# A planned kernel of attention and two MLPs: another DMA model in the planner, other places in the order for weight conversion

## The chip, the cores and the metric

One core of one Trainium2 chip. The time is the device time of one execution in microseconds (us); the median of several executions is compared. The engines are named as the profile names them: PE (TensorE, matmuls), DVE (VectorE), ACT (ScalarE), POOL (GpSimd), SP (SyncE, which here only issues DMAs).

## The reference

Windowed attention over 4 batches, 8 heads, 576 positions, head size 64: heads 0 to 3 see the last 32 positions, heads 4 to 7 every fourth of the last 128. Its output, 2304 tokens by 512, goes through two MLPs:

```python
scores = np.where(masks, scale * np.matmul(q, k.transpose(0, 1, 3, 2)), -1e9)
x = np.matmul(softmax(scores), v)            # (2304, 512) after the heads are joined
h = x @ w_in                                 # first MLP, d_ff 2048
x = (h * np.cos(h)) @ w_out
gate = 1.0 / (1.0 + np.exp(-(x @ w_gate)))   # second MLP, d_ff 1536
out = (gate * (x @ w_val)) @ w_out2
```

The result is float32.

## The kernel before

**Arithmetic.** The matmuls of the MLPs use fp32r operands. A number is split into a high part and a rest, and a product is three matmuls (lines 747 to 749 for the first MLP, 1054 to 1056 and 1202 to 1204 for the second). Weights come as raw bits of wider numbers and are converted on the chip: per weight block of 128x512 a load (403 or 406), ACT's `low` (410) and `mag` (419, or 417 on DVE), then DVE's `shift` (422), `top` (425) and `rnd` (433). For the second MLP there follow, per pair of blocks, four differences on DVE (480, for a scheme that saves one of eight block products), ACT's high part (488), POOL's rest (492) and four DMAs that save the result to DRAM (497). It is read back when its section comes (1029 for gate and value weights, 1188 for the output weights).

**Stages.** The first stage is attention, which feeds the first MLP chunk by chunk (six chunks of 384 tokens). The first MLP has 96 steps: 48 over the first half of d_ff and 48 over the second half, eight steps to a chunk. A step n is the group `h` (12 matmuls into a bank `ps_h`), a chain that alternates between ACT and DVE (`turn` 797 on ACT, `part` 801 on DVE, `cos` 804 on ACT, `g` 807 on DVE, `g_hi` 814 on ACT or 812 on DVE, `g_lo` 817 on DVE), and the group `x2` (12 matmuls into four accumulator banks). After a chunk's last step DVE or ACT takes the four banks out (`x2_take`, 877 on DVE in the second half, 881 and 883 in the first), and only then can the next chunk's first `x2` begin. Weight conversion for the second MLP lies beside these steps. The second MLP has 36 sections, twelve for each pair of chunks; a section has seven products (`p`, into two banks called ps_x, ps_y, ps_z in turn). DVE adds them up in the order u2, u3, vb (1072), gate_b (1083), va (1072) and two `mul` (1090). PE's fourth product waits for u2, its sixth for u3, its seventh for vb, and the next section's first for the bank that gate_b frees. Sums and splits for the output product are DVE's 1161 and 1181.

**What sets the order.** The class `Plan` (lines 55 to 230) is a list scheduler in Python that runs when the kernel is built. Every task has an engine, a duration in ns, dependencies, buffers that it takes and gives, and a priority `prio` in units of steps. The planner plays the tasks through in its own time, an engine that is free takes the ready task of lowest `prio`, and emits each instruction in that order. On the chip each engine, SP too, then works through its queue strictly in that order, and a late instruction holds back all behind it. `port=True` marks tasks that the planner doesn't let run on DVE and POOL at once. `NUDGE` shifts priorities of kinds of tasks while these are under 16 (attention and the first steps). `W_GATE` holds back conversion: gate and value block j may load from step 38 + 1.5 j on, output blocks from step 72 + 1.6 j on (j counted from the first of them). While the first chunk is not yet through, the planner fills idle time of PE with small matmuls, `warm` (1317), of 128x128 bf16; their number is fixed when the kernel is built.

**DMAs in the planner.** Before, some transfers (attention's inputs, raw weights, `x_save`) go through a modelled server `line`, one transfer after another; all others are an SP duration plus a fixed latency, as 3 n ns and 3500 ns for a save of converted weights, or 1460 and 4500 for the read of output weights.

Of the kernel before, what the change touches and what calls it, by code (L numbers as in the profile page):

```python
# [37 lines left out]
SEC = 2.75  # L38
W_PRIO, W_START = 4.5, -4
W_GATE = (12.0, 1.8, 38.0, 1.5, 72.0, 1.6)  # L40
# [6 lines left out]
NUDGE = {"head": 7, "k_out": 1, "load_qk": -0.75, "load_v": -0.75, "p_out": 0.75, "p_transp": -0.5, "pv": -3.5, "s_eps":  # L47
         1, "s_exp": 0.75, "s_max": -0.25, "s_norm": -3.75, "s_rec": 0.5, "scores": 0.5, "w": -0.75, "w_hi": -0.25, "w_load":
         -0.25, "w_mag": 0.5, "w_top": -3.5, "x": 0.75, "x_hi": -1.75}
# [3 lines left out]
class Plan:  # L53
# [18 lines left out]
    DMA_START = 3100  # L72
# [27 lines left out]
    def run(self, start):  # L100
# [35 lines left out]
        while left:  # L136
# [8 lines left out]
            for e in ready:  # L145
# [11 lines left out]
                for k in order:  # L157
# [67 lines left out]
def windowed_attention_mlp_kernel(ctx, tc, q, k, v, w_in, w_out, w_gate, w_val, w_out2, out):  # L225
# [528 lines left out]
    def x_tasks(c):  # L754
# [20 lines left out]
        if c < NC - 2:  # L775
# [4 lines left out]
            add(("x_again", c), "sp", 4400, again, [("x_save", c), prev], begin[s - 1] + 4.0, take=["x"], lat=2200)  # L780
# [84 lines left out]
    def x2_out(s, c, half, n, i):  # L865
# [21 lines left out]
        if half:  # L887
# [5 lines left out]
            add(("x2_load", s, i), "sp", 550, load, [("x2_save", order.index(c), i), "late"] + old, p - 4, take=["o"] if tag == "o" else [], lat=3200,  # L893
# [4 lines left out]
        add(("x2_save", s, i), "sp", 550, lambda: SP.dma_start(out=(x2d if half else x2h)[c][:, i, :], in_=st["o"]),  # L898
            [("x2_take", s, i)], p, give=["o"] if tag == "o" else [], lat=3200 if half else 2200)
# [13 lines left out]
    def xs_tasks(s):  # L913
# [7 lines left out]
        for kk in range(2):  # L921
# [24 lines left out]
            for i, nm in enumerate(("b0", "b1", "a0", "a1")):  # L946
                c, k = (2 * s if nm[0] == "a" else 2 * s + 1), 2 * int(nm[1]) + kk
                deps = [("x2_save", NC + c, k), "late"]
                add(key("xs_load", nm), "sp", 550, lambda nm=nm, f=load: f(nm), deps, base - 1 + i * 0.01, take=["xt"], lat=4200, gate=gate,
# [24 lines left out]
    def xs_wide(s, ca, cb):  # L974
# [22 lines left out]
        for i in range(2):  # L997
            deps = [("x2_save", NC + 2 * s + i, k) for k in range(KD)] + ["late"] + free
            add(("xw_load", s, i), "sp", 1500, lambda i=i: load(i), deps + ([("xw_load", s, 0)] if i else []), base - 1, lat=6000, gate=base - 2)
# [21 lines left out]
    def mlp2_tasks(n):  # L1021
# [9 lines left out]
        for c in (0, 2, 1, 3):  # L1031
# [8 lines left out]
            add(("w2", n, c), "sp", m * 1.5, lambda a=(c, o, m): w_load(*a), deps, p - 2 * SEC + c * 1e-3, lat=2600)  # L1040
# [107 lines left out]
    def out2_tasks(s):  # L1148
# [58 lines left out]
        for j, (nm, _, _) in enumerate(PRODS):  # L1207
            for m in range(NM):
                q = j * NM + m
                whole = end and j == len(PRODS) - 1  # L1210
                if q % 2 == 0:
# [4 lines left out]
                    else:  # L1216
                        deps = [o_key(s, q - 6 + 1)] if g >= 3 else [o_key(s - 1, 42 - 6 + q + 1)] if s else w_saved
                    add(("ow", s, g), "sp", 1460, lambda q=q: w_load(q), deps + [("w2_save", F2 + z, i) for z in range(NM) for i in range(4)],
                        o_pr(q) - (3 if end else 2) * O_LEAD, lat=4500, after=[("ow", s, g - 1)] if g else [])
# [21 lines left out]
                add(("o", s, q), "pe", 9 * 116, lambda a=(j, m): [mm(*a, i) for i in range(TT)], deps, o_pr(q), take=take)  # L1241
            if whole:
                for i in range(TT):
                    deps = [("o_lo", s, nm, m) for m in range(NM)] + [("ow", s, g) for g in range(18, 21)] + [o_key(s, 35 + i)] + (o_read(s, j) if i == 0 else [])
                    add(("o", s, 36 + i), "pe", 18 * 116, lambda i=i: [mm(6, m, i) for m in range(NM)], deps, o_pr(36 + i))
# [14 lines left out]
    def out_tasks(s, j, i, deps, pr):  # L1260
# [30 lines left out]
        if saved:  # L1291
            add(("o_save", s, saved, i), "sp", 550, lambda: save(saved, k), [(what, s, i)], pr, lat=2200)
# [76 lines left out]
```

## Time and profile before

| | |
|---|---|
| median of 3 runs | 946.66 us (943.94 to 952.67) |
| profiled execution | 944.66 us |
| span in the profile | 942.9 us |
| busy PE, DVE, ACT, POOL | 925.6, 718.1, 494.1, 186.7 us |
| PE matmuls | 6952 |
| busy share of the 16 DMA engines, main queue | 72.4% |

A busy time is the sum of an engine's instructions with overlaps counted once. Idle time on PE has a releaser, the instruction for which it waited. A mean duration of a matmul (336 ns for 128x384) is longer than the distance between two starts, since matmuls overlap.

### The profile page before, as it was taken

To read this page: it belongs to the slowest core of one execution; us is meant where nothing else is said; L and a number is where in the kernel's file an instruction comes from. 1 tells how busy PE (TensorE), PEld (TensorE's weight loads), DVE (VectorE), ACT (ScalarE), POOL (GpSimd) and SP (SyncE) were. 2 spreads that over 40 slices of the span, in tenths; PEclk is the share of its full clock that TensorE was granted. 3 is DMA by queue.
4 is the path that set the end of the run, shared out by engine and by line. 5 is a ranking of instruction groups with operands and counts; after the bars stand their busy time and mean duration, and the time that the engine had idled before them with its cause. 6 is when DMAs were issued, how large, how long until landed. Compare 5 with 4: busy or idle time off the path is not lost. (4 is left out here: it accounts for less than half of the span.)

```text
span 942.9 us, 19301 instructions
## 1 busy us (share of the span) xinstructions
PE 925.6 (98%) x6952; PEld 899.9 (95%) x6952; DVE 718.1 (76%) x1720; ACT 494.1 (52%) x1188; POOL 186.7 (20%) x208
## 2 busy tenths in 40 slices
PE   8999999999999999999998999999999999999998
PEld 7889999998999999999998999999999999999998
DVE  6888678787768969998999875776666796566683
ACT  5887678766776466555655522243333253332261
POOL 4434132232223333423422420000000000000000
PEclk9999999999999999999999999999999999999999
DMA  8966545555235699788887698977888987887593
GB/s 194 228 194 183 151 127 152 161 131 145 58 104 178 210 344 335 280 317 297 307 296 236 232 377 294 334 242 238 263 271 274 319 310 244 266 267 215 188 324 109
DMA packets 160911, 221.47 MB, mean 235 GB/s; under 512 B 60592, under 2 KB 126896, under 8 KB 159792
## 3 DMA queue, kind: packets, MB, share of 16 engines
q1 hardware_dynamic: 160016, 220.05, 72.4%
q8 instruction: 55, 0.90, 0.4%
q14 instruction: 40, 0.33, 0.1%
q10 hardware_dynamic: 800, 0.20, 0.1%
HBM read 166.72 MB, written 53.48 MB: 234 GB/s over the span
## 5 line engine op out<-in xcount | busy, mean ns | idle before, releaser
L492 POOL TENSOR_TENSOR lr<-lf,lr 128x512 fp32r<-128x512 f32 (+1 forms) x72 | 92.7, 1306 | 172.0 <-ACT lr L488 159.8
L747 PE MATMUL acc<-gs,arena 128*128 128x384 f32 x240 | 84.8, 353 | 0.9 <-ACT o L883 0.9
L749 PE MATMUL acc<-gs,arena 128*128 128x384 f32 x240 | 80.8, 336 | 0.0
L748 PE MATMUL acc<-gs,arena 128*128 128x384 f32 x240 | 80.6, 336 | 0.0
L1054 PE MATMUL ps_y<-arena 128*128 128x384 f32 x216 | 73.6, 341 | 2.4 <-DVE u L1072 1.8
L1056 PE MATMUL ps_y<-arena 128*128 128x384 f32 x216 | 72.8, 337 | 0.0
L1055 PE MATMUL ps_y<-arena 128*128 128x384 f32 x216 | 72.7, 337 | 0.0
L817 DVE TENSOR_TENSOR gs<-u,gs 128x384 fp32r<-128x384 f32 x96 | 63.7, 666 | 10.3 <-ACT gs L814 9.9
L804 ACT ACTIVATE u<-u 128x384 f32<-128x384 f32 x96 | 49.8, 523 | 40.1 <-DVE u L801 38.8
L797 ACT ACTIVATE r<-ps_h 128x384 int32<-128x384 f32 x96 | 46.4, 483 | 44.4 <-PE ps_h L749 44.0
L747 PE MATMUL ps_h<-arena 128*128 128x384 f32 x192 | 68.4, 356 | 0.6 <-DVE u L807 0.6
L801 DVE SCALAR_TENSOR_TENSOR u<-ps_h,r 128x384 f32<-128x384 f32 x96 | 52.9, 551 | 20.3 <-ACT r L797 19.7
L807 DVE TENSOR_TENSOR u<-ps_h,u 128x384 f32<-128x384 f32 x96 | 52.5, 550 | 17.7 <-ACT u L804 17.4
L749 PE MATMUL ps_h<-arena,wb 128*128 128x384 f32 x192 | 64.7, 337 | 0.0
L748 PE MATMUL ps_h<-arena,wb 128*128 128x384 f32 x192 | 64.7, 337 | 0.0
L747 PE MATMUL ps_h<-arena,wb 128*128 128x384 f32 x192 | 64.7, 337 | 0.0
L749 PE MATMUL ps_h<-arena 128*128 128x384 f32 x192 | 64.5, 336 | 0.0
L748 PE MATMUL ps_h<-arena 128*128 128x384 f32 x192 | 64.4, 335 | 0.0
L1087 ACT ACTIVATE sg<-sg 128x384 f32<-128x384 f32 x36 | 18.9, 525 | 84.3 <-DVE sg L1083 84.3
L410 ACT ACTIVATE wst<-wst 128x512 int32<-128x512 uint32 x68 | 46.1, 677 | 31.0 <-DMA wst<-in_moe_w_val_dram 11.3
L646 ACT ACTIVATE s<-s,mx 128x80 f32<-128x80 f32 (+1 forms) x168 | 59.3, 357 | 0.7 <-DVE mx L639 0.6
L747 PE MATMUL acc<-gs,wb 128*128 128x384 f32 x144 | 49.8, 346 | 4.9 <-DVE lf L877 3.6
(201 smaller groups left out, 2951.3 us busy)
## 6 DMA issues: line engine op xcount, KB each, us to landing
arena<-wd SPq DMA_DIRECT2D x108, 512.0 KB, 4.6
lr<-od SPq DMA_DIRECT2D x42, 512.0 KB, 4.6
wd<-lr SPq DMA_DIRECT2D x36, 512.0 KB, 4.7
wst<-in_moe_w_out_dram SPq DMA_DIRECT2D x28, 512.0 KB, 4.5
arena<-od SPq DMA_DIRECT2D x21, 512.0 KB, 5.6
arena<-wd SPq DMA_DIRECT2D x36, 256.0 KB, 3.9
od<-lr SPq DMA_DIRECT2D x18, 512.0 KB, 4.9
wst<-in_moe_w_in_dram SPq DMA_DIRECT2D x16, 512.0 KB, 4.5
```

The lines of the kernel that those rows point to most:

```text
L492: POOL.tensor_tensor(out=l, in0=x, in1=h.bitcast(F32), op=ALU.subtract)
L646: ACT.activation(out=s, in_=s, func=AF.Exp, scale=-1.0, bias=row("mx", u)[:, i:i + 1], accum_out=row("rs", u)[:, i:i + 1])
L747: PE.matmul(ps, wh, xl, start=first, stop=False)
L748: PE.matmul(ps, wl, xh, start=False, stop=False)
L749: PE.matmul(ps, wh, xh, start=False, stop=last)
L801: DVE.scalar_tensor_tensor(st["u"], st["h"], INV_2PI, st["r"], op0=ALU.mult, op1=ALU.subtract)
L804: ACT.activation(out=st["u"], in_=st["u"], func=AF.Sin, scale=TWO_PI, bias=HALF_PI)
L807: DVE.tensor_tensor(out=st["u"], in0=st["h"], in1=st["u"], op=ALU.mult)
L817: DVE.tensor_tensor(out=st["gs"][:, 1, :], in0=st["u"], in1=st["gs"][:, 0, :].bitcast(F32), op=ALU.subtract)
L1054: PE.matmul(st[to], wh, xl, start=first, stop=False, **more)
L1055: PE.matmul(st[to], wl, xh, start=False, stop=False, **more)
L1056: PE.matmul(st[to], wh, xh, start=False, stop=kk == 1, **more)
```

## The change

All transfers now go through the planner's one server, each with a time by its size, and landing at the earliest `DMA_LEAD` = 2200 ns after its issue plus that time; SP's own cost of an issue is 450 ns everywhere. The first loads keep their formula. Planned durations of the output products rise from 116 to 118.5 ns a matmul. Conversion for the second MLP may start two steps earlier and somewhat closer together. The table of nudges is another. No instruction is added or removed but `warm` matmuls, 267 instead of 298, and a handful of conversion steps that change between ACT and DVE.

```diff
-W_GATE = (12.0, 1.8, 38.0, 1.5, 72.0, 1.6)
+W_GATE = (12.0, 1.8, 36.0, 1.4, 70.0, 1.6)
...
-NUDGE = {"head": 7, "k_out": 1, "load_qk": -0.75, "load_v": -0.75, "p_out": 0.75, "p_transp": -0.5, "pv": -3.5, "s_eps":
...
+NUDGE = {"head": 4.5, "k_out": 0.75, "load_qk": -0.75, "load_v": 3.75, "p_out": -2, "p_transp": -2.5, "pv": -3.75,
...
-    DMA_START = 3100
+    DMA_START, DMA_LEAD = 3100, 2200
+    FIRST_LOADS = ("load_qk", "load_v", "w_load", "x_save")
...
-                        line = max(line, end - t["dma"] + self.DMA_START) + t["dma"]
+                        line = max(line, end + (self.DMA_START - t["dma"] if k[0] in self.FIRST_LOADS else self.DMA_LEAD)) + t["dma"]
...
-            add(("w2_save", nw, z), "sp", 3 * n, lambda a=(k0, k1): save(*a), [("w_blo", nw, z)], pr, lat=3500)
+            add(("w2_save", nw, z), "sp", 450, lambda a=(k0, k1): save(*a), [("w_blo", nw, z)], pr, dma=3 * n)
...
-                        o_pr(q) - (3 if end else 2) * O_LEAD, lat=4500, after=[("ow", s, g - 1)] if g else [])
+                        o_pr(q) - (3 if end else 2) * O_LEAD, dma=1600, after=[("ow", s, g - 1)] if g else [])
...
-                add(("o", s, q), "pe", 9 * 116, lambda a=(j, m): [mm(*a, i) for i in range(TT)], deps, o_pr(q), take=take)
+                add(("o", s, q), "pe", 9 * 118.5, lambda a=(j, m): [mm(*a, i) for i in range(TT)], deps, o_pr(q), take=take)
```

The other changed calls (`x_again`, `x2_load`, `x2_save`, `xs_load`, `xw_load`, `w2`, `o_save`) exchange a duration and `lat` for 450 and `dma` in the same way. In the changed kernel each line after `FIRST_LOADS` stands one further down.

**Place 1: DVE where the last chunk but one ends (steps 88 to 91 of the first MLP).** Line 877 (878 after) takes out the accumulator banks, L801 is `part` of step 90, and after the change L802 is that of step 91. Before:

```order
L801 SCALAR_TENSOR_TENSOR u<-ps_h,r 128x384
L480 TENSOR_TENSOR lf<-lf 128x256
L425 SCALAR_TENSOR_TENSOR wc<-wst,wc 128x512
L480 TENSOR_TENSOR lf<-lf 128x256
L807 TENSOR_TENSOR u<-ps_h,u 128x384
L877 TENSOR_TENSOR lf<-acc_6487,lf 128x384
L877 TENSOR_TENSOR lf<-acc_6494,lf 128x384
L877 TENSOR_TENSOR o<-acc_6498,o 128x384
L877 TENSOR_TENSOR o<-acc_6505,o 128x384
```

After:

```order
L878 TENSOR_TENSOR lf<-acc_6469,lf 128x384
L878 TENSOR_TENSOR lf<-acc_6478,lf 128x384
L481 TENSOR_TENSOR lf<-lf 128x256
L808 TENSOR_TENSOR u<-ps_h,u 128x384
L818 TENSOR_TENSOR gs<-u,gs 128x384
L481 TENSOR_TENSOR lf<-lf 128x256
L939 TENSOR_TENSOR arena<-xt,arena 128x384
L423 TENSOR_SCALAR wc<-wc 128x512
L939 TENSOR_TENSOR arena<-xt,arena 128x384
L802 SCALAR_TENSOR_TENSOR u<-ps_h,r 128x384
L878 TENSOR_TENSOR o<-acc_6484,o 128x384
L878 TENSOR_TENSOR o<-acc_6498,o 128x384
```

The first two takes moved from behind three conversion instructions and `g` of step 90 to right behind `part` of step 90 (the row ahead of those shown); the other two now stand behind `part` of step 91.

**Place 2: DVE between sections 3 and 4 of the second MLP.** The first row is the end of section 3 (`mul`), the L1072 (L1073) is u2 of section 4, for which PE waits. Before:

```order
L1090 TENSOR_TENSOR ub<-u_7405,sg 128x384
L1161 TENSOR_TENSOR ub<-ub 128x384
L1181 TENSOR_TENSOR ur<-ub,ur 128x384
L1161 TENSOR_TENSOR ub<-ub 128x384 x2
L1181 TENSOR_TENSOR arena<-ub,arena 128x384
L1161 TENSOR_TENSOR ub<-ub 128x384
L1072 TENSOR_TENSOR u_7480<-ps_y,s_7458 128x384
```

After:

```order
L1091 TENSOR_TENSOR ub<-u_7380,sg 128x384
L1162 TENSOR_TENSOR ub<-ub 128x384 x2
L1073 TENSOR_TENSOR u_7448<-ps_y,s_7435 128x384
L1073 TENSOR_TENSOR sg<-ps_y,s_7435 128x384
L1182 TENSOR_TENSOR ur<-ub,ur 128x384
L1073 TENSOR_TENSOR vb<-ps_z,sg 128x384
L1162 TENSOR_TENSOR ub<-ub 128x384
L1084 TENSOR_TENSOR sg<-ps_y,s_7435 128x384
```

Of the six sums and splits (1161, 1181) ahead of u2, two are left; the others stand further down, between the additions of section 4.

**Place 3: DVE in section 0, between u2 (the row right ahead of these) and u3 (the L1073 at the end), after the change.** Before, the same stretch held seven conversion instructions and two takes.

```order
L939 TENSOR_TENSOR arena<-xt,arena 128x384
L423 TENSOR_SCALAR wc<-wc 128x512
L939 TENSOR_TENSOR arena<-xt,arena 128x384
L426 SCALAR_TENSOR_TENSOR wc<-wst,wc 128x512
L418 TENSOR_SCALAR wc<-wst 128x512
L434 ISA lf<-wst,wc 128x1024
L423 TENSOR_SCALAR wc<-wc 128x512
L481 TENSOR_TENSOR lf<-lf 128x256
L426 SCALAR_TENSOR_TENSOR wc<-wst,wc 128x512
L481 TENSOR_TENSOR lf<-lf 128x256
L434 ISA lf<-wst,wc 128x1024
L1073 TENSOR_TENSOR sg<-ps_y,s_7063 128x384
```

Nine conversion instructions and two splits now stand ahead of u3, and the takes behind it.

## Rows read from the trace of the kernel before

**Rows 1.** The page, part 1: busy time, share of the span, instructions of each engine

```profile
PE 925.6 (98%) x6952; PEld 899.9 (95%) x6952; DVE 718.1 (76%) x1720; ACT 494.1 (52%) x1188; POOL 186.7 (20%) x208
```

**Rows 2.** Waits of PE over the span: total us, times, longest us

```profile
PE acc L747 <- DVE lf L877: 3.6, 2, 3.3
...
PE ps_y L1054 <- DVE u L1072: 1.8, 1, 1.8
...
PE acc L747 <- ACT o L883: 1.5, 2, 0.9
PE acc L747 <- DVE o L881: 0.7, 1, 0.7
```

**Rows 3.** Windows: busy us of each engine by stretch, granted clock, DMA share

```profile
core 0: us, PE busy (x) PEld busy (x) DVE busy (x) ACT busy (x) POOL busy (x), PEclk, DMA share, GB/s
...
60.00:80.00 20.00, 20.00 (x209) 18.95 (x207) 18.73 (x48) 18.30 (x50) 8.77 (x9) 1.00 0.50 138
...
505.00:510.00 5.00, 4.00 (x15) 4.00 (x16) 3.87 (x9) 3.46 (x8) 1.84 (x2) 0.66 0.67 246
```

**Rows 4.** Timeline of PE, 45 to 48 us: start, duration, line, operation, count

```profile
45.96 1.45 PE L1317 MATMUL acc<-identb 128*128 128x128 bf16 x23
47.25 0.50 PE L597 MATMUL ps_t<-ident,k 96*128 96x96 f32 x4
```

**Rows 5.** Timeline of PE, 500 to 509 us

```profile
500.49 0.34 PE L747 MATMUL ps_h<-arena,wb 128*128 128x384 f32 x1
...
502.40 0.34 PE L749 MATMUL ps_h<-arena,wb 128*128 128x384 f32 x1
506.00 0.69 PE L747 MATMUL acc<-gs,wb 128*128 128x384 f32 x1 [3.26 <-DVE lf L877]
...
509.00 0.34 PE L747 MATMUL acc<-gs,wb 128*128 128x384 f32 x1
```

**Rows 6.** Timeline of DVE, 501 to 515 us

```profile
501.50 0.41 DVE L480 TENSOR_TENSOR lf<-lf 128x256 f32<-128x256 f32 x1
501.84 1.78 DVE L425 SCALAR_TENSOR_TENSOR wc<-wst,wc 128x512 int32<-128x512 int32 x1
503.54 1.48 DVE L480 TENSOR_TENSOR lf<-lf 128x256 f32<-128x256 f32 x1
...
505.40 1.01 DVE L877 TENSOR_TENSOR lf<-acc,lf 128x384 f32<-128x384 f32 x2
...
514.91 0.68 DVE L425 SCALAR_TENSOR_TENSOR wc<-wst,wc 128x512 int32<-128x512 int32 x1
```

**Rows 7.** Timeline of POOL, 500 to 507 us

```profile
501.59 5.25 POOL L492 TENSOR_TENSOR lr<-lf,lr 128x512 fp32r<-128x512 f32 x4 [11.51 <-ACT lr L488]
```

**Rows 8.** Timeline of PE, 567 to 574 us

```profile
567.91 0.34 PE L1056 MATMUL ps_x<-arena 128*128 128x384 f32 x1
570.04 0.44 PE L1054 MATMUL ps_y<-arena 128*128 128x384 f32 x1 [1.79 <-DVE u L1072]
...
573.80 0.34 PE L1054 MATMUL ps_y<-arena 128*128 128x384 f32 x1
```

**Rows 9.** Timeline of DVE, 566 to 570 us

```profile
566.33 0.55 DVE L1161 TENSOR_TENSOR ub<-ub 128x384 f32<-128x384 f32 x1
...
569.44 0.55 DVE L1072 TENSOR_TENSOR u<-ps_y,s 128x384 f32<-128x384 f32 x1
```

**Rows 10.** Timeline of PE and, under it, of DVE before 558 us

```profile
555.13 0.34 PE L1056 MATMUL ps_z<-arena 128*128 128x384 f32 x1
557.28 0.44 PE L1054 MATMUL ps_x<-arena 128*128 128x384 f32 x1 [1.81 <-DVE sg L1083]
...
555.14 1.62 DVE L1161 TENSOR_TENSOR ub<-ub 128x384 f32<-128x384 f32 x1
556.69 0.54 DVE L1083 TENSOR_TENSOR sg<-ps_y,s 128x384 f32<-128x384 f32 x1
```

**Rows 11.** The page, part 6: DMA issues, median us from issue to landing

```profile
lr<-od SPq DMA_DIRECT2D x42, 512.0 KB, 4.6
```

More of the change, by code (lines that the diff above doesn't have):

```diff
@@ L46 @@
 NUDGE_UNTIL = 16
-NUDGE = {"head": 7, "k_out": 1, "load_qk": -0.75, "load_v": -0.75, "p_out": 0.75, "p_transp": -0.5, "pv": -3.5, "s_eps":
-         1, "s_exp": 0.75, "s_max": -0.25, "s_norm": -3.75, "s_rec": 0.5, "scores": 0.5, "w": -0.75, "w_hi": -0.25, "w_load":
-         -0.25, "w_mag": 0.5, "w_top": -3.5, "x": 0.75, "x_hi": -1.75}
+NUDGE = {"head": 4.5, "k_out": 0.75, "load_qk": -0.75, "load_v": 3.75, "p_out": -2, "p_transp": -2.5, "pv": -3.75,
+         "q_out": -0.5, "s_eps": 2.75, "s_exp": 1, "s_max": -1, "s_norm": -1.25, "s_rec": 3.5, "scores": -4.5, "transp": -0.25,
+         "w_hi": -0.25, "w_load": 0.5, "w_mag": 2, "w_rnd": -0.5, "x": -10.25, "x_hi": -3.75, "x_save": -8.5}
 WARM, WARM_NS = 1200, 57
@@ L779, in x_tasks @@
             prev = ("x_again", order[s - 1]) if s > NC + 2 else ("x_new", NC - 1)
-            add(("x_again", c), "sp", 4400, again, [("x_save", c), prev], begin[s - 1] + 4.0, take=["x"], lat=2200)
+            add(("x_again", c), "sp", 450, again, [("x_save", c), prev], begin[s - 1] + 4.0, take=["x"], dma=4600)
         add(("x_free2", c), None, 0, nothing, [("h", last, KD - 1)], give=["x"])
@@ L892, in x2_out @@
                 xr_slots.append(("x2_save", s, i))
-            add(("x2_load", s, i), "sp", 550, load, [("x2_save", order.index(c), i), "late"] + old, p - 4, take=["o"] if tag == "o" else [], lat=3200,
+            add(("x2_load", s, i), "sp", 450, load, [("x2_save", order.index(c), i), "late"] + old, p - 4, take=["o"] if tag == "o" else [], dma=600,
                 after=xr_prev("x2_load", s, i))
@@ L897, in x2_out @@
             give=["acc" if i < 3 else "accw"])
-        add(("x2_save", s, i), "sp", 550, lambda: SP.dma_start(out=(x2d if half else x2h)[c][:, i, :], in_=st["o"]),
-            [("x2_take", s, i)], p, give=["o"] if tag == "o" else [], lat=3200 if half else 2200)
+        add(("x2_save", s, i), "sp", 450, lambda: SP.dma_start(out=(x2d if half else x2h)[c][:, i, :], in_=st["o"]),
+            [("x2_take", s, i)], p, give=["o"] if tag == "o" else [], dma=600)
     order2 = order[NC:]
@@ L948, in xs_tasks @@
                 deps = [("x2_save", NC + c, k), "late"]
-                add(key("xs_load", nm), "sp", 550, lambda nm=nm, f=load: f(nm), deps, base - 1 + i * 0.01, take=["xt"], lat=4200, gate=gate,
+                add(key("xs_load", nm), "sp", 450, lambda nm=nm, f=load: f(nm), deps, base - 1 + i * 0.01, take=["xt"], dma=600, gate=gate,
                     after=prev + ([key("xs_load", ("b0", "b1", "a0")[i - 1])] if i else []))
@@ L998, in xs_wide @@
             deps = [("x2_save", NC + 2 * s + i, k) for k in range(KD)] + ["late"] + free
-            add(("xw_load", s, i), "sp", 1500, lambda i=i: load(i), deps + ([("xw_load", s, 0)] if i else []), base - 1, lat=6000, gate=base - 2)
+            add(("xw_load", s, i), "sp", 450, lambda i=i: load(i), deps + ([("xw_load", s, 0)] if i else []), base - 1, dma=2400, gate=base - 2)
         loads = [("xw_load", s, 0), ("xw_load", s, 1)]
@@ L1039, in mlp2_tasks @@
                 deps.append(("h", (begin[2 * NC - 1] if c else NSTEP) - 1, KD - 1))
-            add(("w2", n, c), "sp", m * 1.5, lambda a=(c, o, m): w_load(*a), deps, p - 2 * SEC + c * 1e-3, lat=2600)
+            add(("w2", n, c), "sp", 450, lambda a=(c, o, m): w_load(*a), deps, p - 2 * SEC + c * 1e-3, dma=m * 1.5)
         def mm(j, kk):
@@ L1217, in out2_tasks @@
                         deps = [o_key(s, q - 6 + 1)] if g >= 3 else [o_key(s - 1, 42 - 6 + q + 1)] if s else w_saved
-                    add(("ow", s, g), "sp", 1460, lambda q=q: w_load(q), deps + [("w2_save", F2 + z, i) for z in range(NM) for i in range(4)],
-                        o_pr(q) - (3 if end else 2) * O_LEAD, lat=4500, after=[("ow", s, g - 1)] if g else [])
+                    add(("ow", s, g), "sp", 450, lambda q=q: w_load(q), deps + [("w2_save", F2 + z, i) for z in range(NM) for i in range(4)],
+                        o_pr(q) - (3 if end else 2) * O_LEAD, dma=1600, after=[("ow", s, g - 1)] if g else [])
                 k = slots[q % len(slots)]
@@ L1244, in out2_tasks @@
                     deps = [("o_lo", s, nm, m) for m in range(NM)] + [("ow", s, g) for g in range(18, 21)] + [o_key(s, 35 + i)] + (o_read(s, j) if i == 0 else [])
-                    add(("o", s, 36 + i), "pe", 18 * 116, lambda i=i: [mm(6, m, i) for m in range(NM)], deps, o_pr(36 + i))
+                    add(("o", s, 36 + i), "pe", 18 * 118.5, lambda i=i: [mm(6, m, i) for m in range(NM)], deps, o_pr(36 + i))
             for i in range(TT):
@@ L1291, in out_tasks @@
         if saved:
-            add(("o_save", s, saved, i), "sp", 550, lambda: save(saved, k), [(what, s, i)], pr, lat=2200)
+            add(("o_save", s, saved, i), "sp", 450, lambda: save(saved, k), [(what, s, i)], pr, dma=400)
     xy, zz = {}, {}
```

## The prediction

> **What bounds the kernel now.** I read the busy times first: PE works in 98% of the span, DVE in 76%, ACT in 52% [rows 1]. The change takes away no work of DVE or ACT, and of PE only filler, so it can gain just what PE loses: 17.3 us of idle time in the span (942.9 less 925.6), some filler, and time at a lower clock. The waits of PE then show for whom it idles [rows 2]: for accumulator banks that DVE takes out (3.6 us) or ACT and DVE in the first half (1.5 and 0.7), and for u2 in the second MLP (1.8). No DMA is among the large ones. Nearly all of it lies in few places, and I read those in the timelines.
>
> Place 1, at 506 us. PE's last matmul of step 91's `h` starts at 502.40, its next at 506.00 [rows 5]. The usual distance is 1.91 / 11 = 0.174 us (from 500.49 to 502.40), so 506.00 - 502.57 = 3.43 are lost. The following nine matmuls take 3.00 us to the next start at 509.00 instead of 9 x 0.174 = 1.57: the granted clock in that stretch is 0.66 on average, so part of it ran at 1.2 GHz instead of 2.4, right after the idle time [rows 3]. Together 4.9 us. The take came at 505.40 because two conversion instructions ahead of it lasted 1.78 and 1.48 us [rows 6], where the same forms take 0.68 and 0.41 elsewhere in these rows. POOL ran four of its 128x512 subtractions from 501.59 for 5.25 us [rows 7]. So some 2.2 of the 3.4 us is DVE held up beside POOL, and the rest is DVE's order.
>
> Place 2, at 570 us. PE stands from 568.08 to 570.04 (1.96), and its next twelve matmuls take 3.76 us to 573.80 instead of 2.09 [rows 8]: together 3.6 us. DVE does six sums and splits from 566.33 before it reaches u2 at 569.44 [rows 9]. POOL has finished by then; this is order alone.
>
> At 557 us PE loses 557.28 - 555.30 = 2.0 us behind gate_b, which stood behind a sum of 1.62 us against 0.55 for the same form in [rows 9], again beside POOL [rows 10]. The two waits for ACT and DVE in the first half's takes [rows 2] sum to 2.2, of which I count 1.3 at the change from the first to the second half of d_ff and 0.9 earlier. That makes 12.7 us in named places. The rest of the idle time is the first wait of the program, the tail, and pieces under 0.7.
>
> **What the change does, term by term.** I start from the profiled execution, 944.66 us (span 942.9 and 1.8 around it).
>
> Filler: 31 `warm` matmuls fewer. They stand in PE's own queue and are executed whatever happens, at 1.29 / 23 = 0.056 us each [rows 4]: -1.7 us, if nothing else makes PE wait there. That holds the planner's word that attention runs more tightly; the bounds are 0, if DVE is late by as much, and -1.7.
>
> Place 1: the first two takes now stand right behind `part` of step 90. In before's times that is at about 501 and the banks are complete by then, so both are done by 502.5, when PE needs the first. The other two stand behind `part` of step 91. From the end of `part` of step 90 DVE has the two takes, `g`, `g_lo`, two splits and `part` (7 x 0.47, the distance of such instructions, as 3.11 / 6 = 0.5 in [rows 9] shows with short gaps) and three short ones (0.34 each, [rows 6]): 4.3 us, so the third take would run from 505.8 to 506.3. PE has two groups of step 88 and three of step 92's `h` meanwhile (5 groups of 3 x 0.174 = 0.52, to 505.2), and would wait 1.1. If `part` isn't late as it was before, no wait stays; a meeting with POOL adds 1.1. I take 1.0 where 4.9 was: -3.9 (bounds -4.9 and 0).
>
> Place 2: two sums instead of six instructions ahead of u2 take 0.94 us instead of 3.1, which is 2.2 less than now, more than the 1.96 that PE waits. The four others go between the additions of section 4, one at a time, 0.47 each, beside products of 1.04 us on PE. So the wait goes, and the low clock with it: -3.6 (bounds -3.6 and -1.0).
>
> At 557 the order is nearly as before; whether DVE meets POOL there is open. I take half: -1.0 (bounds -2.0 and 0). At the change of halves the order now has two groups of step 52's `h` between the second and third take instead of behind the third: -0.6 (bounds -1.3 and 0).
>
> New costs. (a) In section 0, nine conversion instructions and two splits, 4 x 0.60 + 5 x 0.34 + 2 x 0.47 = 5.0 us, stand ahead of u3, where 4.1 us stood. PE needs u3 after 14 groups behind the second product's (7.3 us); u3 ends 0.7 + 5.0 + 0.5 = 6.2 us after it. The slack of 1.1 us covers one meeting with POOL, not two: +0.5 (bounds 0 and 3.7, a wait of 2.0 and a low clock as in place 2). (b) At the end of the chunk before (step 80), DVE's takes come a step later; the planner sends two `h` groups ahead on PE. Counted as in place 1, the first take ends about 0.5 us after PE needs it: +1.0 with half a meeting (bounds 0 and 3.3, for two meetings and the clock). (c) In the attention stage two more conversion instructions lie ahead of step 9, and DVE is busy 18.73 of 20 us from 60 to 80 [rows 3]: +0.5 (bounds 0 and 3). (d) The planner now lets a read of 512 KB output weights land 0.45 + 2.2 + 1.6 - 0.45 = 3.8 us after its issue, where the trace has 4.6 [rows 11] and before the planner had 4.5 behind an issue of 1.46. Three slots of buffers cover most of that 0.8 us: +0.5 (bounds 0 and 2).
>
> Sum: 944.66 - 1.7 - 3.9 - 3.6 - 1.0 - 0.6 + 0.5 + 1.0 + 0.5 + 0.5 = 936.4. The median of the three runs shown is 946.66, 2.0 above the profiled execution, and I carry that over: **938.4 us**, 0.9% less.
>
> How a meeting with POOL is priced matters for five of these terms. The rows give 1.07 (1.48 less 0.41) and 1.10 (1.78 less 0.68). The Trainium skill, in "SBUF — State Buffer", section "Who interferes with whom", says that the pair of ports which DVE shares with POOL is held for a whole instruction and the other engine blocks fully, also for a DVE instruction with two SBUF inputs. By that rule a meeting costs at most one POOL instruction, 5.25 / 4 = 1.3 us, and the half meetings in the sum would make it 0.3 us more; the trace agrees with the kind of delay, at 1.1.
>
> **Rivals.**
> 1. *All waits go.* For it: each named wait has a cause in the order, and the new order breaks up the two longest. Against it: meetings with POOL aren't planned, they come from drift, in any order. 944.66 - 1.7 - 12.7 = 930.3, as a median 932.
> 2. *The waits move.* The last conversions still end in section 2, at the same place as before: 33 conversion instructions lie behind step 90 instead of 32. If DVE is late by 2 to 3 us somewhere else, with the low clock behind it, two such places cost 3.6 to 4.9 each, as much as places 1 and 2 gave. Then only filler and small waits are gained: 944.66 - 1.7, and 1.6 less at the small places, is 941.4 to 943.0, as a median 943 to 945.
> 3. *Slower.* POOL's meetings fall on section 0, where u3 has 1.1 us of slack. One mechanism: each long wait there or at a chunk's end costs 3.6 to 4.9 us with its clock; before has two. All old ones gone leave 930.3; four new ones at 4.2 give 947, the point from which it is slower; seven would be needed for 1%. The Trainium skill's rule, in the section named above, that whichever instruction starts first holds the pair, speaks for this: the planner can't steer who is first once the engines drift.
>
> **How the numbers follow.** My forecast (936 to 941 as a median) 0.45, rival 1 0.17, rival 2 0.27, rival 3 0.11. A measurement can tell about 1% from no change. Faster by over 1%, below 937.2, is rival 1 and some four tenths of the forecast: 0.17 + 0.19 = 0.36. Slower by over 1% is half of rival 3: 0.06. Within 1%: 0.58. The range reaches from rival 1's 932, less 1 for its spread, to 948, which leaves out the upper part of rival 3 and the lower edge of rival 1.
>
> **What would show it.** In the profile after: PE's idle time near 10 us instead of 17.3; 267 matmuls of line 1318; no wait for line 878 above 1.5 us and none for u2 (line 1073) of 1.8; granted clock 1.00 in all stretches of 5 us behind the chunk's end and section 3. Wrong steps would show as a new wait of PE for DVE of 2 us or more with a clock of about 0.66 behind it, at step 80, in section 0, or before step 12, or as waits for DMA under lines 1203 to 1205. The forecast falls if such waits sum to more than 8 us, or if the first 100 us aren't shorter by about 1.7.

## The result, and the profile after

The changed kernel takes 935.85 us (median of 4 executions, 934.83 to 937.71), the kernel before beside it 947.03 (943.94 to 952.67): a ratio of 0.9878, with a 95% interval of 0.9828 to 0.9927. On another chip, in six executions, it is 935.41 us and 0.9875 (0.9846 to 0.9903). The forecast was 938.4 us, in a range of 931 to 948. The profiled execution took 936.45 us, with a span of 934.7.

All rows of the kernel after stand one line further down (L878 for 877, L1073 for 1072). The page, part 1, against [rows 1]:

```profile
PE 919.7 (98%) x6921; PEld 893.9 (96%) x6921; DVE 723.4 (77%) x1722; ACT 495.3 (53%) x1186; POOL 187.8 (20%) x208
```

The waits of PE over the span, against [rows 2] (total us, times, longest us):

```profile
PE acc L748 <- DVE o L878: 1.7, 1, 1.7
...
PE ps_h L748 <- DVE u L808: 1.5, 1, 1.5
...
PE ps_y L1055 <- DVE u L808: 0.9, 1, 0.9
```

The take at place 1 costs one wait of 1.7 where it cost 3.3, u2 (L1073) isn't among the large waits any more, and gate_b's 1.8 at 557 is gone. PE's matmuls number 31 fewer. Its idle time is 934.7 - 919.7 = 15.0 us against 17.3.

Windows of the kernel after, against [rows 3] (us, PE, PEld, DVE, ACT, POOL busy, granted clock, DMA share, GB/s):

```profile
505.00:510.00 5.00, 4.50 (x25) 4.50 (x26) 5.00 (x11) 2.19 (x5) 0.00 (x0) 1.00 0.74 258
560.00:565.00 5.00, 5.00 (x29) 4.69 (x28) 3.39 (x7) 2.05 (x5) 0.00 (x0) 1.00 1.03 413
```

The granted clock is 1.00 behind the chunk's end and behind section 3, where it was 0.66 in 505 to 510 before; only the last 3 us, in which PE has no matmul any more, show less (0.91).

Place 1 after. DVE's timeline, with POOL's two instructions of that stretch and PE's wait under it, against [rows 5 to 7]:

```profile
499.01 1.00 DVE L878 TENSOR_TENSOR lf<-acc,lf 128x384 f32<-128x384 f32 x2
...
501.20 1.51 DVE L481 TENSOR_TENSOR lf<-lf 128x256 f32<-128x256 f32 x1
...
503.44 1.08 DVE L939 TENSOR_TENSOR arena<-xt,arena 128x384 fp32r<-128x384 f32 x1
...
504.91 1.00 DVE L878 TENSOR_TENSOR o<-acc,o 128x384 f32<-128x384 f32 x2
```

```profile
501.14 1.29 POOL L493 TENSOR_TENSOR lr<-lf,lr 128x512 fp32r<-128x512 f32 x1 [2.94 <-ACT lr L489]
503.29 0.81 POOL L493 TENSOR_TENSOR lr<-lf,lr 128x256 fp32r<-128x256 f32 x1 [0.86 <-ACT lr L489]
```

```profile
505.50 0.44 PE L748 MATMUL acc<-gs,wb 128*128 128x384 f32 x1 [1.69 <-DVE o L878]
```

The first two takes run at 499.01, 2 us before PE's first matmul of the next chunk into these banks, at 501.05. Eight other instructions stand between them and the third take; two of them lie beside POOL and last 1.51 instead of 0.41 and 1.08 instead of 0.55. That is 1.6 us, and PE waits 1.7.

Place 2 after, DVE's timeline, against [rows 9], and PE's:

```profile
561.57 1.14 DVE L1162 TENSOR_TENSOR ub<-ub 128x384 f32<-128x384 f32 x2
562.63 0.55 DVE L1073 TENSOR_TENSOR u<-ps_y,s 128x384 f32<-128x384 f32 x1
```

```profile
562.91 0.34 PE L1057 MATMUL ps_x<-arena 128*128 128x384 f32 x1
563.24 0.44 PE L1055 MATMUL ps_y<-arena 128*128 128x384 f32 x1
```

Two sums stand ahead of u2 instead of six instructions, and PE's fourth product of section 4 starts 0.33 us after the matmul before it, where 0.17 is usual, instead of the 1.96 us of standing in [rows 8].

**Where the time went, stretch by stretch.** The stretches run from the start of PE's first matmul of one group to that of another, in the profiled executions of before, after, and a second run of after (span 932.8). The last columns are differences from before; the predicted one puts the prediction's terms into the same stretches.

```
stretch                                      before   predicted   after   second
start to step 40 (filler, term c)            284.01     -1.2      -0.85   -1.45
step 40 to 49 (change of halves)              53.97     -0.6      +0.61   -0.98
step 49 to the first x2 of step 72             96.96      0        -1.08   -1.08
to the first x2 of step 81 (term b)           38.45     +1.0      +0.31   +0.33
to the first x2 of step 89 (place 1)          38.20     -3.9      -3.39   -3.40
sections 0 and 1 (term a)                     36.30     +0.5      +1.42   +1.32
section 2 (the wait at 557)                    9.39     -1.0      -1.62   -1.60
sections 3 and 4 (place 2)                    18.61     -3.6      -3.77   -3.73
the rest (term d)                            363.44     +0.5      +0.18   +0.56
sum                                                     -8.3      -8.19  -10.03
```

### The profile page after: what moved, and what is told of

It reads as the page before. It is cut to its first block, busy times and chain, and to the rows that moved or that the text cites. A ratio compares the mean times of both kernels' runs of the same rounds, so it can differ in the third digit from the quotient of the medians.

```text
span 934.7 us, 19268 instructions
## 1 busy us (share of the span) xinstructions
PE 919.7 (98%) x6921; PEld 893.9 (96%) x6921; DVE 723.4 (77%) x1722; ACT 495.3 (53%) x1186; POOL 187.8 (20%) x208
## 4 chain that ended last, share of the span: by engine, by line
PE 78%; DVE 9%; DMA 6%; ACT 3%; issue 3%; SPq 0%; POOL 0%; ACTq 0%; DVEq 0%
PE ps_h L748 6%; PE acc L748 5%; PE ps_h L750 5%; PE ps_h L749 5%; PE acc L750 5%; PE acc L749 5%; PE ps_y L1055 4%; PE ps_y L1057 4%; PE ps_y L1056 4%; PE xy L1203 3%; PE xy L1205 3%; PE xy L1204 3%; PE ps_x L1055 2%; PE ps_x L1057 2%; PE ps_z L1055 2%
## 5 line engine op out<-in xcount | busy, mean ns | idle before, releaser
L493 POOL TENSOR_TENSOR lr<-lf,lr 128x512 fp32r<-128x512 f32 x72 | 93.2, 1307 | 168.4 <-ACT lr L489 157.8
L818 DVE TENSOR_TENSOR gs<-u,gs 128x384 fp32r<-128x384 f32 x96 | 67.5, 704 | 9.1 <-ACT gs L815 8.3
L802 DVE SCALAR_TENSOR_TENSOR u<-ps_h,r 128x384 f32<-128x384 f32 x96 | 52.9, 551 | 16.3 <-ACT r L798 15.6
```

Source lines behind the costliest of these rows:

```text
L802: DVE.scalar_tensor_tensor(st["u"], st["h"], INV_2PI, st["r"], op0=ALU.mult, op1=ALU.subtract)
L818: DVE.tensor_tensor(out=st["gs"][:, 1, :], in0=st["u"], in1=st["gs"][:, 0, :].bitcast(F32), op=ALU.subtract)
```

## The experiments

Of the changed lines three parts can be exchanged apart: the table of nudges (with the number of fillers that follows from it), `W_GATE`, and the DMA model (with the 118.5 ns). Other kernels keep the planner of before, let it finish its order, and then move single tasks in it; their lines stand 14 to 21 further down, as each text says.

**Place 2 alone.** The kernel before, with this added behind the finished order:

```diff
+MOVES = [
+    (('o_lo', 0, 'a0', 0), 'after', ('u3', 4)),
+    (('o_sum', 0, 's2', 0), 'after', ('vb', 4)),
+    (('o_lo', 0, 'a0', 1), 'after', ('gate_b', 4)),
+    (('o_sum', 0, 's2', 1), 'after', ('va', 4)),
+]
```

> The kernel before with one edit: of the six sums and splits that DVE has ahead of u2 of section 4, the last four stand between the additions of section 4 (behind u3, vb, gate_b, va), as in the changed kernel; every other queue is the same. If order alone made the wait at 570 us, PE's wait there of 1.96 and the twelve slow matmuls behind it (1.67) go: 3.6 us less than before. If the four only make another addition late, a wait of 1 to 2 us appears in section 4 or 5 and the gain is under 1.5 us.

Measured: a ratio of 0.9984 (0.9958 to 1.0009), 946.39 us against 947.77. In its trace the place is mended: sections 3 and 4 take 15.17 us instead of 18.61, which is the predicted 3.4 to 3.6. PE's fourth product (lines 18 further down) waits for a DMA, and only 0.18:

```profile
567.34 0.41 PE L1072 MATMUL ps_y<-arena 128*128 128x384 f32 x1 [0.18 <-DMA arena<-wd]
```

The times allow -4.0 to +0.9 us. The place doesn't cost 3.6 in every execution: in two of the other traces with the old order there (nudges alone and POOL later, below) a wait of 2.0 leaves the clock at 1.00, and the place costs 2.0. And other waits differ by 2 us from one execution to another, place 1's among them. So this run bears out the mechanism in the trace, and the times can't tell 3.6 from 2 or from nothing.

The same trace shows something of place 1, where nothing was moved: up to there every engine's queue is that of before. POOL's timeline, DVE's and PE's (lines 18 further down):

```profile
505.80 6.39 POOL L510 TENSOR_TENSOR lr<-lf,lr 128x512 fp32r<-128x512 f32 x4 [11.45 <-ACT lr L506]
```

```profile
506.06 0.69 DVE L443 SCALAR_TENSOR_TENSOR wc<-wst,wc 128x512 int32<-128x512 int32 x1
```

```profile
508.07 0.44 PE L765 MATMUL acc<-gs,wb 128*128 128x384 f32 x1 [1.21 <-DVE lf L895]
```

Here the meeting with POOL went the other way. POOL's four subtractions take 6.39 us instead of the 5.25 of [rows 7], DVE's conversion step lasts 0.69 instead of 1.78, and PE waits 1.21 instead of 3.26. Four traces have before's queues of all engines at this place: in two DVE is held up (PE waits 3.26 in before and 3.42 with less filler), in two POOL is (1.21 here and 1.18 with the nudges alone). So the 4.9 us that the prediction read at place 1 are not lost in every execution.

**Place 1 alone.** The kernel before with the four takes and `g` of step 90 moved ahead of two differences and a conversion step (lines 21 further down):

```diff
+    (('x2_take', 10, 0), 'after', ('cos', 90)),
...
+    (('g', 90), 'after', ('x2_take', 10, 3)),
+    (('w_sum', 14, 2), 'after', ('g', 90)),
+    (('w_top', 62), 'after', ('w_sum', 14, 2)),
```

> The kernel before with one edit: DVE does the four takes of the accumulator banks and g of step 90 before two differences (480) and one conversion step (425), which follow; every other queue is the same. If PE's wait at 506 us comes from what stands ahead of the takes, it goes with its slow matmuls: 4.0 to 4.9 us less than before. If DVE's total work beside POOL is what binds there, the same instructions make g_lo of step 89 or part of step 91 late by some 2 us, PE waits 2 to 3 us a step later, and the gain is under 2 us.

Measured: 0.9999 (0.9973 to 1.0025), no gain. The trace shows where the gain went. The stretch of place 1 takes 33.35 us instead of 38.20, as expected. But everything behind it is 4 to 5 us earlier and meets POOL elsewhere. DVE's timeline at step 95, with PE's wait and the windows behind it:

```profile
519.66 1.66 DVE L959 TENSOR_TENSOR arena<-xt,arena 128x384 fp32r<-128x384 f32 x1
521.24 1.51 DVE L501 TENSOR_TENSOR lf<-lf 128x256 f32<-128x256 f32 x1
```

```profile
525.00 0.44 PE L1075 MATMUL ps_y<-arena 128*128 128x384 f32 x1 [1.90 <-DVE u L828]
```

```profile
525.00:530.00 5.00, 5.00 (x20) 5.00 (x21) 3.65 (x8) 1.84 (x3) 0.00 (x0) 0.66 0.07 27
555.00:560.00 5.00, 4.57 (x17) 4.58 (x18) 2.42 (x5) 1.02 (x2) 0.49 (x1) 0.66 0.97 373
```

In before PE waited 0.6 for this `g` of step 95. Now it is 1.90, and some of the next 5 us run at 1.2 GHz (granted clock 0.66 on average), and the wait of 1.8 at 555, which kept the full clock before, is followed by such a stretch too. Sections 0 to 2 take 50.25 us instead of 45.69: 4.6 us are given back. That is rival 2, the waits move, for a change made at one place alone.

**POOL later.** The kernel before, its takes in their old places, but ACT's high parts, on which POOL's four subtractions at 501.59 wait [rows 7], behind `turn` of step 91:

```diff
+    (('w_bhi', 14, 0), 'after', ('turn', 91)),
+    (('w_blo', 14, 0), 'after', ('w_bhi', 14, 0)),
+    (('w2_save', 14, 0), 'after', ('w_blo', 14, 0)),
+    (('w_bhi', 14, 1), 'after', ('w2_save', 14, 0)),
...
+    (('w_bhi', 14, 3), 'after', ('w_bhi', 14, 2)),
```

> The kernel before with one edit: ACT makes the four high parts of the block converted at 501 us (488) only behind turn of step 91, so that POOL's four subtractions run after DVE's takes and not beside the conversion steps ahead of them; DVE's and PE's queues are the same. If the meeting with POOL costs DVE 2.2 us ahead of the takes, DVE's 425 and 480 there last about 0.68 and 0.41 again, PE's wait falls from 3.4 to about 1.2 us, the clock stays at 1.00 and the time falls by 3 to 3.7 us. If DVE's order alone makes the wait, it stays at 3 us or more and the time is that of before.

Measured: 0.9962 (0.9939 to 0.9985), 3.75 us less in the medians, as the theory of the meeting says. DVE's queue is that of before, instruction by instruction. POOL's timeline, and DVE's (lines 21 further down):

```profile
504.87 5.27 POOL L513 TENSOR_TENSOR lr<-lf,lr 128x512 fp32r<-128x512 f32 x4 [14.27 <-ACT lr L509]
```

```profile
502.34 0.69 DVE L446 SCALAR_TENSOR_TENSOR wc<-wst,wc 128x512 int32<-128x512 int32 x1
502.94 0.42 DVE L501 TENSOR_TENSOR lf<-lf 128x256 f32<-128x256 f32 x1
...
503.75 1.01 DVE L898 TENSOR_TENSOR lf<-acc,lf 128x384 f32<-128x384 f32 x2
...
506.50 1.78 DVE L454 CUSTOM_DVE_ANT_0 lf<-wst,wc 128x1024 uint16<-128x1024 uint16 x1
```

The two conversion instructions that lasted 1.78 and 1.48 in [rows 6] last 0.69 and 0.42. The meeting now falls behind the takes, on a conversion instruction for which nobody waits. PE waits 1.23 instead of 3.26, which is DVE's order without POOL, and the clock stays at 1.00. The trace alone wouldn't show that the move did it, since the same wait of 1.2 stands in two traces without the move; the times show it, with an interval that lies wholly below 1.

**Less filler.** The kernel before, with every fifth filler behind the 133rd left out (265 instead of 298):

```diff
-        if cold():
+        if cold() and (i < 133 or i % 5):
```

> The kernel before with 33 of its 298 filler matmuls (1317) left out, one in five of those after the first 133; nothing else changes. If filler costs its time in PE's queue, as the prediction has it, 33 x 0.056 = 1.8 us less. If PE has to wait there for DVE or ACT anyway, the time falls by under 0.5 us and PE's idle time in the first 80 us grows by about as much as filler goes.

Measured: 1.0024 (0.9996 to 1.0051), no gain; the rival holds. Windows from 0 to 60 us, this kernel and under it before:

```profile
0.00:60.00 60.00, 53.42 (x760) 47.41 (x761) 46.32 (x207) 41.54 (x140) 26.80 (x52) 1.00 0.92 219
```

```profile
0.00:60.00 60.00, 56.17 (x790) 50.12 (x790) 46.85 (x209) 42.04 (x142) 27.11 (x52) 1.00 0.91 220
```

PE is busy for 2.8 us less and stands for 2.8 us more. Filler that isn't there becomes waiting for DVE, ACT and DMA.

**The three parts, one at a time and in pairs.** Each is one or two lines of the diff ahead of the prediction.

> The kernel before with the new table of nudges alone: the queues differ in attention and the first steps only (DVE's first 500 instructions of 1660), with 267 filler matmuls. As in the prediction: 1.7 us less filler, 0.5 us of new waits, so 1.2 us less than before. If the stage waits for DVE and ACT in either order, 0 to 0.5 us less. Places 1 and 2 keep their waits of 3.4 and 2.0 us.

> The kernel before with the earlier start of conversion alone (the new W_GATE): DVE's queue differs from row 1060 to 1200 only. All four takes of the chunk's end at step 88 come right behind part and g of step 90, so the wait at place 1 goes (up to 4.9 us less); ahead of u2 of section 4 stand a take, two splits and a sum instead of six, so about half of place 2's wait stays, without the slow clock: together 6 to 8 us less. If the conversions had only moved their load elsewhere, a new wait of 2 us or more shows at steps 84 to 95 or in section 0, and it is under 4 us less.

> The kernel before with the new model of the transfers alone (one server, 450 ns to issue, 118.5 instead of 116 ns for the output products): DVE's queue differs from row 300 on. The takes of step 88 come in two pairs right behind part and g, so place 1 goes; ahead of u2 of section 5 stand four sums and splits, so some of the wait of place 2 stays: 5 to 8 us less than before. If the changed kernel's gain comes from the places of the conversions and not from the transfers' model, under 3 us less.

> The change with the old table of nudges, so with 298 filler matmuls; behind the attention stage every queue has the order of the changed kernel. Theory (the gain is made by the conversion's new places together with the new DMA model, and the nudges give nothing, as they gave nothing alone): 9 to 12 us under the kernel before, a ratio of 0.987 to 0.990, and the time of place 1 and of section 3 to 4 as in the changed kernel (third take 1 to 2 us late, no wait for u2). Rival (the 31 fillers are worth what they take in PE's queue, 1.7 us, once nothing later eats it): 1.7 us over the changed kernel, a ratio near 0.990 to 0.992.

> The change with conversion at its old places (the old W_GATE); nudges and DMA model are new. Theory (the DMA model alone mends sections 3 to 5 and the change of halves, and leaves the takes at step 88 behind three DVE instructions that meet POOL): 4 to 6 us under the kernel before, a ratio of 0.994 to 0.996, with a PE wait of 3 us or more for the first take of the last chunk but one. Rival (the parts simply add up, and the nudges cost the 2 us that they cost alone): 2 to 3 us under it, 0.997 to 0.998.

> The change with the old DMA model; nudges and the conversion's places are new. Theory (conversion earlier puts the reads of the gate and value weights behind saves in SP's queue that wait for DVE, which only the new model orders otherwise): a PE wait of 3 us or more for a read of these weights in sections 3 to 5 with 1.2 GHz behind it, and 5 to 8 us over the kernel before, a ratio of 1.005 to 1.009. Rival (that wait came from where the engines had drifted in one execution, not from the order): no DMA wait above 1 us, and within 2 us of the kernel before.

> The changed kernel itself, so that the three others have it beside them on the same chip and in more executions. By its first executions: 934.8 to 938 us, a ratio of 0.986 to 0.990. If the kernel before has a wide spread because its takes meet POOL or don't, the changed kernel's executions stay within 4 us of each other and those of the kernel before spread over 9 us or more.

Measured, with the spread of each kernel's executions, and from each trace three stretches of the table above: steps 40 to 81, place 1, sections 3 and 4.

```
new parts         ratio to before (95%)      median, us (spread)        40-81   place 1   3 and 4
none                                         947.77 (941.18 to 954.67)  189.38   38.20    18.61
nudges            1.0030 (0.9999 to 1.0062)  947.78 (943.22 to 954.41)  195.38   35.75    18.58
gate              1.0073 (1.0045 to 1.0101)  951.62 (950.87 to 957.10)  190.44   40.08    21.33
DMA model         0.9950 (0.9929 to 0.9972)  940.89 (940.07 to 943.26)  187.71   38.83    14.97
nudges, gate      1.0056 (1.0033 to 1.0079)  953.44 (948.06 to 957.40)  189.82   41.05    20.47
nudges, DMA       0.9915 (0.9884 to 0.9947)  939.84 (938.06 to 940.63)  187.71   38.70    14.97
gate, DMA         0.9888 (0.9859 to 0.9918)  937.21 (934.29 to 938.54)  188.13   34.81    14.85
all three         0.9875 (0.9846 to 0.9903)  935.41 (934.63 to 937.38)  187.65   34.80    14.88
```

The ratios of one call share the executions of before on that chip; the first row is from one of three calls (medians 947.77, 945.75, 947.71). Four things follow.

First, the DMA model is the one part that gains alone, about 5 of the 12 us, and earlier conversion has the sign that the DMA model gives it. With the old model it makes the kernel slower by 0.7%; with the new one it makes it faster, by 4.4 us on one chip (939.84 without the gate, 935.41 with it, and the executions of the two don't overlap). For the gate alone I had expected a gain, wrong by sign. For the DMA model alone I had expected 5 to 8 us and no wait at place 1; it gained just under 5, and the wait there is 3.65. What was expected of the kernel without the DMA model held. The nudges gained nothing alone, and in their trace place 1 has a wait of 1.18 where 3.4 was expected. Without them the change is 1.8 us slower, which is the rival's distance at the theory's ratio, and the intervals overlap, so whether they give nothing or 2 us stays open. The kernel without the gate came out better than either expectation (0.9915), though its wait for the first take is there as foreseen, 3.2 us; the parts don't add up.

Second, why the gate alone is slower. PE's timeline in section 4 with the gate alone (lines as before), with the window behind it:

```profile
566.23 0.66 PE L1054 MATMUL ps_y<-arena 128*128 128x384 f32 x1 [3.47 <-DMA arena<-wd]
```

```profile
565.00:570.00 5.00, 3.77 (x12) 3.80 (x13) 1.28 (x3) 0.00 (x0) 0.00 (x0) 0.54 0.97 370
```

PE waits for a read of gate and value weights. SP's timeline shows the read late in its queue:

```profile
550.02 2.84 SPq L1029 DMA_DIRECT2D arena<-wd  x2
553.33 0.77 SPq L497 DMA_DIRECT2D od<-lr  x1
...
555.97 2.65 SPq L497 DMA_DIRECT2D od<-lr  x3
...
561.76 0.32 SPq L898 DMA_DIRECT2D x2d<-lf  x1
562.13 1.40 SPq L1029 DMA_DIRECT2D arena<-wd  x3
```

From 552.9 to 562.1 SP issues no read of these weights. Saves and reloads stand ahead that wait for POOL, for another DMA and for DVE's take; the last of them, at 561.76, for the take. In the changed kernel SP issues a read at 553.75 and the next six from 556.18, a gap of 2.1 us. With nudges and gate but the old model the wait comes back, at 3.95 us. So it comes with the order and is not one execution's drift.

Third, place 1. With only one of gate and DMA model, nudges or not, the take waits 2.5 to 3.7 us behind DVE instructions beside POOL. DVE, POOL and PE with the DMA model alone (lines one further down):

```profile
500.31 1.78 DVE L426 SCALAR_TENSOR_TENSOR wc<-wst,wc 128x512 int32<-128x512 int32 x1
502.02 1.63 DVE L939 TENSOR_TENSOR arena<-xt,arena 128x384 fp32r<-128x384 f32 x1
503.57 1.75 DVE L434 CUSTOM_DVE_ANT_0 lf<-wst,wc 128x1024 uint16<-128x1024 uint16 x1
...
505.71 1.01 DVE L878 TENSOR_TENSOR lf<-acc,lf 128x384 f32<-128x384 f32 x2
```

```profile
500.07 5.84 POOL L493 TENSOR_TENSOR lr<-lf,lr 128x512 fp32r<-128x512 f32 x4 [13.22 <-ACT lr L489]
```

```profile
506.31 0.44 PE L748 MATMUL acc<-gs,wb 128*128 128x384 f32 x1 [3.65 <-DVE lf L878]
```

Three meetings of about 1.1 us each make most of a wait of 3.65.

Fourth, steps 40 to 81. The eight traces with the old DMA model (the four of the table and the four of the kernels above) take 188.9 to 195.4 us there, on average 191.0; the six with the new one (the four of the table, the first of the changed kernel, and the kernel of the next part) 187.3 to 189.2, on average 188.0. That is 3 us, of which the first profile of before showed only 1.4. What differs is ACT. Its waits for raw weights (`low`) from 285 to 475 us, before and under it after:

```profile
ACT wst L410 <- DMA wst<-in_moe_w_val_dram: 11.3, 9, 1.8
ACT wst L410 <- DMA wst<-in_moe_w_gate_dram: 3.8, 5, 1.8
ACT wst L410 <- DMA wst<-in_moe_w_out_dram: 2.9, 3, 1.4
```

```profile
ACT wst L411 <- DMA wst<-in_moe_w_val_dram: 2.6, 2, 1.6
ACT wst L411 <- DMA wst<-in_moe_w_gate_dram: 0.9, 3, 0.3
ACT wst L411 <- DMA wst<-in_moe_w_out_dram: 0.8, 1, 0.8
```

It is 18.0 us in 17 waits against 4.3 in 6; the DMA model alone has 5.0, the nudges alone 17.4. The planner of before let loads and saves pass each other in its time, took the loads for landed earlier than they were, by these waits, and put `low` into ACT's queue ahead of the steps' `turn` and `cos`. Each such wait holds back the chain of a step. That these waits cause PE's is argued from the kernels in which both come and go together; no run takes away one of them alone.

**A better order.** The kernel after, with five more moves, taken from the waits in its trace (lines 19 further down):

```diff
+    (('g', 50), 'before', ('w_sum', 2, 3)),
+    (('x2_take', 5, 2), 'after', ('w_bhi', 2, 3)),
+    (('x2_take', 10, 2), 'after', ('g_lo', 89)),
+    (('x2_take', 10, 3), 'after', ('x2_take', 10, 2)),
+    (('p', 0, 1, 0), 'after', ('x2', 93, 1)),
```

> The changed kernel with five single moves at the waits that its trace shows: g of step 50 ahead of a difference, the third take of the chunk before step 48 earlier on ACT, the third and fourth takes at step 88 behind g_lo of step 89, and PE's first group of section 0's second product behind two groups of step 93. If each wait is due to what stands ahead of it, 1.7, 1.7 and 0.9 us go: 3 to 4.3 us less than the changed kernel, some 931 us. If DVE, ACT or the landing of the saved banks bind there, the waits reappear within a step and it is under 1.5 us less.

Measured: 934.43 us (933.53 to 937.12), a ratio to before of 0.9889 (0.9860 to 0.9917). That is 1.0 us under the six executions of the changed kernel, which ran on another chip, less than either's spread, and by the ratio to before (0.9889 against 0.9875) it isn't ahead at all. So no gain can be told; the other expectation, that the waits reappear, holds. Its trace has what was meant. Place 1 takes 32.83 us instead of 34.81, and no take or `g` waits for over 0.5 us. Of these 2.0 us 1.7 are given back at once: sections 0 to 2 take 47.22 instead of 45.49, with new waits of PE in section 0, 1.1 us for a split of L958 and 1.0 for u2 or u3 (L1092).

## Why the prediction was right, point by point

**Place 2** came out as worked: u2 is met in time, and the stretch is 3.8 us shorter where 3.6 stood. The kernels with one part tell that the DMA model did it; the nudges and the gate leave it as it was or add the DMA wait.

**Place 1**: -3.9 forecast, -3.4 measured. The cause named, DVE held up beside POOL, is shown by the run that only moves POOL. The size holds for the profiled execution of before alone: with the same queues the stretch took 34.9 us in the trace of the run on place 2, as short as the 34.8 of the changed kernel, because there POOL was held up and not DVE. Against that outcome the changed order gives 0.1 us, against the other 3.4; how often before has either is not known. The remaining wait is 1.7 where I took 1.0: one meeting more (1.1) would have made it 2.1. The order moved the third take as read, but not far enough.

**557 us**: I took half of 2.0 us; 1.6 went. **Section 0**: u3, for which I counted 1.1 us of slack, makes no wait over 0.35. The loss of 1.3 to 1.4 comes in pieces, the largest the wait of 0.9 for `g` of step 95 among the rows above. The term was of the right kind and 0.9 too small. **Step 80**: +1.0 forecast, +0.3 measured; no meeting fell on it.

**Filler**: -1.7 less 0.5 forecast, -0.85 and -1.45 measured. The working was wrong, though, in holding that each filler costs what it takes. Without 33 of them PE stands instead. Seven traces with all fillers reach step 40 at 284.4 us on average (282.98 to 285.77), six with the nudges at 283.5 (282.56 to 285.20). That is 0.9 us, less than the spread of either.

**The change of halves**: -0.6 forecast, +0.6 in one trace of the changed kernel and -1.0 in the other. In both a difference ahead of `g` of step 50 lasts 1.5 us beside POOL, but PE waits for that `g` 1.5 in the first and 0.25 in the second: that `g` starts 12.6 us after PE's first matmul of step 49 in the first and 11.3 in the second. Such a term has no sign from one profile.

**What was left out**: the steps 49 to 72. I costed the new DMA model only as a risk, by the reads of output weights (+0.5, and hardly so much came of it). Its gain, ACT no longer standing before loads, was not in my sum: -1.1 by the first profile, some -3 for steps 40 to 81 on average. The rows were there; I read PE's waits and not ACT's, which stands between DVE's instructions of each step.

**The carry to the median** is the mis-sized term. The sum gave 936.4 for the profiled execution, which took 936.45. That it fits so closely is luck: its terms are off by as much as 1.2 us, some up and some down, one of -1.1 is missing, and the second profiled execution gained 1.7 more than the sum. I added 2.0 because before's median lay 2.0 above its profile. But the kernel before spreads over 9 to 13 us, and the changed one over 3. With the new DMA model the median lay within 1 us of the profiled execution. Its own median was 935.85, so the carry should have been nothing. So the measured median lies just below the 936 to 941 in which I counted the forecast, and a gain of over 1%, as this one is, had a chance of only 0.36. Before's profiled 944.66 is one of its better executions, and part of the gain, some 3 of 11 us, is that its worse ones are gone; why they are is not shown, beyond place 1.

**The signs.** 267 matmuls of line 1318, no u2 wait, and a full clock behind both places hold. No new wait of 2 us came. PE's idle time, forecast near 10 us, is 15.0; that figure didn't follow from my own sum, since filler (1.7) and slow matmuls (3.1) are busy time: 17.3 - (8.3 - 4.8) = 13.8. The wait for L878 is 1.7 where I said none over 1.5, and the first stretches are shorter by 0.9 to 1.5, not 1.7.

## What to carry to other kernels

A planner's model of transfers can show its errors on the engine that takes the loaded data: look for waits of that engine on DMA, even where PE waits for no DMA at all. Then the parts of a plan are tried together and not only one by one, since one part's sign can hang on another. And where a kernel's executions spread over 1%, one profile is one draw: the stretches of several traces with the same queues tell which wait is always there. Place 1's was not: the same queues gave 1.2 or 3.3 us.

## What the runs showed of the hardware

**Which DVE instructions POOL holds up.** In the kernel after, from 285 to 560 us, by line (ns, min/median/max):

```profile
L802 DVE SCALAR_TENSOR_TENSOR u<-ps_h,r x56: 542/549/560, 286.1 to 522.2; 128x384 f32<-128x384 f32 x56
...
L878 DVE TENSOR_TENSOR lf<-acc,lf x14: 541/546/558, 363.5 to 548.3; 128x384 f32<-128x384 f32 x14
L818 DVE TENSOR_TENSOR gs<-u,gs x57: 542/555/1655, 288.1 to 527.9; 128x384 fp32r<-128x384 f32 x57
L481 DVE TENSOR_TENSOR lf<-lf x72: 408/418/1521, 298.2 to 550.2; 128x256 f32<-128x256 f32 x72
L426 DVE SCALAR_TENSOR_TENSOR wc<-wst,wc x37: 674/683/1784, 284.5 to 540.3; 128x512 int32<-128x512 int32 x37
```

`part` and the takes, which read one operand from a bank, never last over 0.56 us, nor does `g`; 39 of these lay for at least three quarters of their time beside a POOL instruction. The three others, whose operands are all in SBUF, are drawn out by up to 1.1 us. That DVE is held up and not POOL is not settled by the order of the queues, as the two outcomes at place 1 show. A take may stand beside POOL; what must not stand ahead of it there is a split or a conversion. The Trainium skill has a rule for this ("SBUF — State Buffer", section "Who interferes with whom"): a DVE instruction with at most one SBUF input, outside its modes with two ports, does not contend with GpSimd. The trace agrees: none of these 39 lasted more than 0.56 us. I had priced meetings by the half of that rule that speaks of two SBUF inputs, and not used this one, by which an order can be mended.

**The clock after a wait.** A long wait of PE was not always followed by the lower of the two levels, 1.2 GHz. In the kernel with less filler the take of place 1 comes 3.42 us late, and the granted clock stays at full speed, where before showed 0.66 behind 3.26 us [rows 3]:

```profile
510.00:515.00 5.00, 2.92 (x16) 2.92 (x17) 4.96 (x9) 3.66 (x9) 2.93 (x3) 1.00 0.43 170
```

At place 2 the clock fell behind a wait of 1.79 us in the kernel before and behind one of 2.03 with the takes of place 1 moved; behind 2.00 with POOL later and 2.03 with the nudges alone it did not. The length of the wait alone doesn't decide it, and what does stays open. A wait of 2 us is therefore worth 2.0 or 3.6, and two kernels that differ by one such wait can differ by either.
